# Weight pieces fetched three ahead of a conversion with two VectorE passes, in an attention and two-layer feed-forward kernel

## The chip, the cores and the metric

The kernel runs on one core of a Trainium2 chip. The metric is the device time of one execution in microseconds; lower is better. Three executions of the kernel before took 1069.86 to 1070.5 us, median 1070.43.

## The reference

The inputs are float32 for attention and float64 for the weights, as `_moe_setup` draws them (a float32 array divided by a numpy float64 scalar).

```python
scores = np.where(causal, -1e9, scale * q @ k.T)
a = np.exp(scores - scores.max(-1)); a /= a.sum(-1) + 1e-9
local = a @ v
q_p = phi(q)                                  # relu-like, elu(x) + 1
mem_out = (q_p @ M_prev) / (q_p @ z_prev + 1e-6)
x = g * mem_out + (1 - g) * local             # B=4, H=8, S=576, D=64
h = x @ w_in;  y = (h * cos(h)) @ w_out       # 2304 x 512, d_ff = 2048
h = y @ w_in2; out = (h * tanh(softplus(h))) @ w_out2
```

## The kernel before, in words

Attention is done for 16 pairs of heads (batch b, pair p), each in five steps of 128 rows of queries. A step has three stages that run two steps apart: `stage_a` (scores `sp` on TensorE for each of the two heads, mask and row maximum on VectorE at L240, exponential on ACT at L243, scaling on GpSimd at L265), `stage_b` (transposes `tp` and their copies `aT`) and `stage_c` (the sum `o`, whose high and low part go to DRAM as xsH and xsL). Both heads of a pair use one half of TensorE's rows each for `sp` and one half of its columns each for `o`. `prep` loads q, k, v and the memory of the next pair; `memory` makes the products `mp` and `mo`.

The feed-forward layers use products with high and low parts, three matmuls for one. Each layer's hidden width is cut into two halves, each half's weights stay in SBUF as float32r pairs: w0 (first layer, first half), w1, then w2 and w3 for the second layer. `ffn` alternates `first` (products `h`, L420) and `second` (products `y`, L478, L487). For the first half of the first layer, 256 tokens at a time, this work is spread over attention from the second batch on (L573 to L577), and x is read back from DRAM by `load_block` in tiles xbH and xbL.

The weights come as raw 8-byte numbers, in pieces of 128 x 512 (512 KB), 16 pieces for a half. `to_f32` (L121) loads a piece into one of two buffers `wst` and makes float32 of its two words, `lo` and `hi`: GpSimd scales `hi` (L119), ACT makes the three bits of `lo` (L128), and three VectorE passes put them together (L129, L130, L133). Then `load_half` (L146) makes the high part (`wh`, ACT or GpSimd in turn) and the low part (L163, GpSimd or VectorE in turn). `converted` (L556) takes the 16 pieces of w0 one after the other from attention step CONV0 = 14 on, 0.9 a step; the other 48 go beside the feed-forward stages.

The order on each engine is not the program's order: the tile framework lists the instructions by its own timeline when the kernel is built, and `tc.issue_after` holds some of them behind a marked instruction. SP issues all transfers from one queue, and one that waits for a free buffer holds up all behind it.

## Time and profile before

| what | value |
|---|---|
| median of 3 runs | 1070.43 us (1069.86 to 1070.5) |
| profiled execution, first to last instruction | 1068.0 us |
| around the span, median less span | 2.4 us |
| TensorE busy | 1042.6 us, 98% |
| VectorE, ACT, GpSimd busy | 490.7, 485.8, 391.6 us |
| moved by DMA | 116.99 MB, 110 GB/s over the span |

The profiled execution's own time is its span and the 2.4 us around it, 1070.4 us. Idle time of an engine counts only where TensorE, which is busy nearly always, waits for it. A group of instructions is named by source line, engine, operation and tiles; a mean can mix shapes.

### The profile page before, as it was taken

The numbers are of one execution on the slowest core, as the hardware profiler recorded it, in microseconds if no ns is written. First come the engines' busy times: TensorE is split into PE (matmuls) and PEld (weight loads), VectorE is DVE, ScalarE is ACT, GpSimd is POOL, SyncE is SP. The second block draws the span as 40 slices with busy tenths as digits, with TensorE's granted clock in tenths as the row PEclk, the third lists the DMA queues.
The fourth block names the chain that finished last, engine by engine and source line by source line (L and its number), as shares of the span: only waits on it lengthen the run. The fifth ranks groups of instructions, "written<-read, shape, count | busy, mean of one in ns | idle before, by whom it ended". The sixth has DMA issues, their size and how long they took to land.

```text
span 1068.0 us, 17139 instructions
## 1 busy us (share of the span) xinstructions
PE 1042.6 (98%) x6512; PEld 873.7 (82%) x6512; DVE 490.7 (46%) x1136; ACT 485.8 (45%) x1023; POOL 391.6 (37%) x425
## 2 busy tenths in 40 slices
PE   6997999999999999999999999999999999999998
PEld 4666688787878899998888889888888888888897
DVE  4588885445554558776766655665000000000000
ACT  6797875556564534344535454543322321222131
POOL 3377853323232334555555555654101010110100
PEclk8999999999999999999999999999999999999999
DMA  6366642323121275425345355630300300110010
GB/s 235 119 196 224 205 135 82 119 83 122 59 87 46 73 266 190 139 90 198 110 166 177 111 176 185 228 119 22 116 1 1 118 1 0 60 40 1 21 41 20
DMA packets 66369, 116.99 MB, mean 110 GB/s; under 512 B 5616, under 2 KB 25072, under 8 KB 66288
## 3 DMA queue, kind: packets, MB, share of 16 engines
q1 hardware_dynamic: 66288, 115.91, 32.2%
q8 instruction: 51, 0.84, 0.3%
q14 instruction: 30, 0.25, 0.1%
HBM read 87.58 MB, written 28.31 MB: 109 GB/s over the span
## 4 chain that ended last, share of the span: by engine, by line
PE 92%; ACT 2%; DVE 2%; DMA 2%; issue 1%; POOL 1%; SPq 0%; DVEq 0%; POOLq 0%; ACTq 0%
PE h L420 37%; PE y L478 20%; PE y L487 18%; PE o L324 5%; PE sp L238 4%; PE tp L297 4%; PE o L313 2%; PE mp L277 1%; PE sp L251 1%; DMA qt<-in_qp_dram 1%; DMA wst<-in_w1i_dram 1%; DVE at L240 1%; ACT at L243 1%; DMA vt<-in_vn_dram 1%; POOL at L265 0%
## 5 line engine op out<-in xcount | busy, mean ns | idle before, releaser
L420 PE MATMUL h<-xbH,w 128*128 128x256 f32 (+1 forms) x1536 | 393.0, 338 | 0.1
L420 PEld LDWEIGHTS h<-xbH,w 128*128 128x128 f32 x1536 | 266.9, 190 | 33.7 <-issue 1.0
L420 PE MATMUL h<-xbL,w 128*128 128x256 f32 (+1 forms) x768 | 258.0, 336 | 1.5 <-DMA xbL<-xsL 1.5
L478 PE MATMUL y<-g,w 128*128 128x256 f32 (+1 forms) x1344 | 221.5, 319 | 4.4 <-ACT aT L115 4.2
L478 PEld LDWEIGHTS y<-g,w 128*128 128x128 f32 x1344 | 193.1, 192 | 30.8 <-issue 9.4
L487 PE MATMUL y<-w,g 128*128 128x512 f32 x864 | 201.8, 389 | 0.0
L487 PEld LDWEIGHTS y<-w,g 128*128 128x128 f32 x864 | 161.9, 188 | 33.5
L392 DVE TENSOR_TENSOR g<-e,g 128x512 fp32r<-128x512 f32 x36 | 24.9, 691 | 297.1 <-ACT g L115 297.1
L420 PEld LDWEIGHTS h<-xbL,w 128*128 128x128 f32 x768 | 145.6, 190 | 16.9 <-DMA xbL<-xsL 1.7
L392 POOL TENSOR_TENSOR g<-e,g 128x512 fp32r<-128x512 f32 x36 | 47.8, 1328 | 286.5 <-ACT g L115 286.5
L265 POOL TENSOR_SCALAR at<-at,sm,omg 128x128 f32<-128x128 f32 (+2 forms) x144 | 102.7, 723 | 134.4 <-DVE sm L263 119.2
L384 ACT ACTIVATE e<-h 128x512 f32<-128x512 f32 x72 | 43.0, 597 | 232.5 <-PE h L420 231.0
L392 POOL TENSOR_TENSOR g<-u,g 128x512 fp32r<-128x512 f32 x72 | 102.0, 1436 | 121.5 <-ACT g L115 45.6
L367 ACT ACTIVATE u<-h 128x512 int32<-128x512 f32 x72 | 42.9, 595 | 111.9 <-PE h L420 104.2
L243 ACT ACTIVATE at<-at,mn 128x128 f32<-128x128 f32 (+3 forms) x128 | 70.9, 555 | 28.2 <-DVE mn L240 26.8
L129 DVE SCALAR_TENSOR_TENSOR wst<-wst 128x512 int32<-128x512 int32 x64 | 53.9, 843 | 37.7 <-POOL wst L119 31.3
L119 POOL TENSOR_SCALAR wst<-wst 128x512 f32<-128x512 f32 x64 | 46.4, 731 | 63.2 <-DMA wst<-in_w1i_dram 25.1
L297 PE MATMUL tp<-ident,at 128*128 128x128 f32 x384 | 63.9, 285 | 5.6 <-DVE den L281 2.2
L368 DVE SCALAR_TENSOR_TENSOR u<-u,h 128x512 f32<-128x512 int32 x72 | 49.0, 682 | 40.8 <-ACT u L367 40.5
L240 DVE CUSTOM_DVE_ANT_0 at<-sp,mask 128x128 f32<-128x128 f32 (+3 forms) x128 | 59.3, 482 | 17.6 <-PE sp L238 16.0
L133 DVE TENSOR_TENSOR wst<-wst 128x512 int32<-128x512 int32 x64 | 66.1, 1035 | 1.2
L324 PE MATMUL o<-aT,vt 128*64 128x128 f32 (+1 forms) x896 | 64.5, 272 | 1.7 <-ACT aT L115 1.5
(76 smaller groups left out, 1084.1 us busy)
## 6 DMA issues: line engine op xcount, KB each, us to landing
wst<-in_w1i_dram SPq DMA_DIRECT2D x16, 512.0 KB, 5.4
wst<-in_w1o_dram SPq DMA_DIRECT2D x16, 512.0 KB, 4.6
wst<-in_w2i_dram SPq DMA_DIRECT2D x16, 512.0 KB, 4.0
wst<-in_w2o_dram SPq DMA_DIRECT2D x16, 512.0 KB, 4.7
qd<-in_qT_dram SPq DMA_DIRECT2D x16, 320.0 KB, 3.4
vt<-in_vn_dram SPq DMA_DIRECT2D x16, 320.0 KB, 3.2
xbH<-xsH SPq DMA_DIRECT2D x20, 256.0 KB, 4.9
xbL<-xsL SPq DMA_DIRECT2D x20, 256.0 KB, 4.6
```

The costliest lines, as they stand in the source:

```text
L129: nc.vector.scalar_tensor_tensor(lo, hi, 3, lo, ALU.logical_shift_left, ALU.bitwise_or)
L133: nc.vector.tensor_tensor(dst, lo, hi, ALU.bitwise_xor)
L240: nc.vector.tensor_tensor_reduce(at[:, :N], sp[:, :N], mask[:, SM - q0:SM - q0 + N], SSC, 3.0e38, ALU.add, ALU.min, mn[:, j:j + 1])
L243: marks["act"] = nc.scalar.activation(at[:, :N], at[:, :N], AF.Exp, bias=mn[:, j:j + 1], scale=-1.0, accum_out=sm[:, j:j + 1]).ins
L265: turn_of("sc", b == 0).tensor_scalar(at[:, :N], at[:, :N], sm[:, j:j + 1], gates[j], ALU.mult, ALU.mult)
L297: nc.tensor.transpose(tp[:, c:c + P], at[:, c:c + P], ident)
L324: marks["pe"] = nc.tensor.matmul(o[j * D:(j + 1) * D, :n], st["vt"][:kk, c, j * D:(j + 1) * D], a, start=False, stop=c == i, skip_group_ch ...
L368: nc.vector.scalar_tensor_tensor(u, u.bitcast(I32), -TWO_PI, h, ALU.mult, ALU.add)
L392: turn_of(kind).tensor_tensor(gL, g, gH.bitcast(F32), ALU.subtract)
L420: nc.tensor.matmul(h[:, a * T:(a + 1) * T], w_[:, c, f0:f0 + P], x_[c], start=m == 0, stop=m == 3 * NC - 1)
L478: nc.tensor.matmul(y[e // per][:, cols], w_[:, f, es], g_, start=fst and m == 0 and e % per == 0, stop=lst and m == 2, skip_group_check=True)
L487: nc.tensor.matmul(y[t], g_[:, tsl], w_[:, f, :], start=fst and m == 0, stop=lst and m == 2, skip_group_check=True)
```

## The change

A piece is now fetched by `fetch` and converted by `to_f32`, and the generator of `load_half` runs three pieces ahead with its fetches; `wst` has four buffers. Fetches of w0 may start from attention step LOAD0 = 9. ACT's pass becomes a scaled copy that leaves the rounding in range without a clamp, and VectorE needs two passes: one takes the sign bit of `hi` into `lo`, one shifts `hi` by three and joins it. For w1 nothing is fetched ahead; for w2 three fetches stand at the start of the second half. The tiles xbH and xbL of the 256-token blocks become one ring of four places each (before, three buffers each), and 16 one-element memsets of the weight tiles go, with the constant 7.

```diff
@@ -19,11 +19,12 @@
 TWO_PI = 2.0 * math.pi
 BIG = 8.0e9
 BUFS = dict(
-    mb=2, kd=4, qd=4, aD=4, vt=2, qt=1, ph=2, den=2, mo=4, xH=1, xL=3, sm=7, mn=2, at=8, aT=7, u=2, e=3, g=4, h=4, y=4, xb=3, yp=3, yh=2, yl=2, wst=2, S=6, T=8,
+    mb=2, kd=4, qd=4, aD=4, vt=2, qt=1, ph=2, den=2, mo=4, xH=1, xL=3, sm=7, mn=2, at=8, aT=7, u=2, e=3, g=4, h=4, y=4, xb=3, xbH=4, xbL=4, yp=3, yh=2, yl=2, wst=4, S=6, T=8,
 )
 RES = 2
-TOUCH = 1
 CONV0 = 14
+LOAD0 = 9
+AHEAD = 3
 CONVR = 0.9
 PACE1 = 1.5
 PREP = 3
@@ -38,6 +39,7 @@
 
 
 REBIAS = 2.0 ** -112
+LOW = 29.0 / 32.0
 
 
 @with_exitstack
@@ -98,10 +100,16 @@
     nc.vector.reciprocal(gate, igate)
     nc.vector.tensor_scalar(omg, gate, -1.0, 1.0, ALU.mult, ALU.add)
 
-    c_seven = const.tile([P, 1], F32, name="c_seven")
-    nc.gpsimd.memset(c_seven, 7.0)
-
     counts = {}
+    rings = {}
+
+    def ring(pool, tag, shape, dtype=F32):
+
+        if tag not in rings:
+            rings[tag] = [pool.tile([shape[0], BUFS[tag], *shape[1:]], dtype, name=tag), 0]
+        r = rings[tag]
+        r[1] += 1
+        return r[0][:, (r[1] - 1) % BUFS[tag]]
 
     def turn_of(kind, first=False):
         kind += "0" if first else ""
@@ -118,20 +126,19 @@
         else:
             eng.tensor_scalar(dst, src, scale, 1.0, ALU.mult, ALU.mult)
 
-    def to_f32(src, dst=None):
-
-
+    def fetch(src):
         st = wk.tile([P, SM, 2], I32, tag="wst", name="wst", bufs=BUFS["wst"])
         nc.sync.dma_start(st, src)
+        return st
+
+    def to_f32(st):
+
         lo, hi = st[:, :, 0], st[:, :, 1]
         scaled("ws", hi.bitcast(F32), hi.bitcast(F32), REBIAS)
-        nc.scalar.activation(lo, lo.bitcast(U32), AF.Relu, scale=-(2.0 ** -29), bias=c_seven)
+        nc.scalar.activation(lo, lo.bitcast(U32), AF.Copy, scale=LOW * 2.0 ** -29, bias=0.2495)
+        nc.vector.scalar_tensor_tensor(lo, hi, -(1 << 31), lo, ALU.bitwise_and, ALU.bitwise_or)
         nc.vector.scalar_tensor_tensor(lo, hi, 3, lo, ALU.logical_shift_left, ALU.bitwise_or)
-        nc.vector.tensor_scalar(hi, hi, -(1 << 31), 7, ALU.bitwise_and, ALU.bitwise_or)
-        if dst is None:
-            dst = lo
-        nc.vector.tensor_tensor(dst, lo, hi, ALU.bitwise_xor)
-        return dst.bitcast(F32)
+        return lo.bitcast(F32)
 
     def weight_pieces(win, wout, half, tl):
 
@@ -143,15 +150,20 @@
         for f in range(f0 // P, f0 // P + 2):
             yield wo[:, f]
 
-    def load_half(pool, tagp, source, kind):
+    def load_half(pool, tagp, win, wout, half, kind, ahead=AHEAD):
         tiles = []
         for tl in range(NTL):
             tiles.append([pool.tile([P, NC, SM // 2] if k < 2 else [P, 2, DM], F32R, tag=f"{tagp}{k}{tl}", bufs=1,
                                     name=f"{tagp}{k}{tl}") for k in range(4)])
+        todo = [(tl, n, src) for tl in range(NTL) for n, src in enumerate(weight_pieces(win, wout, half, tl))]
 
         def gen():
-            for tl in range(NTL):
-                for n, t in enumerate(source(tl)):
+            raw = {}
+            for i in range(-ahead, len(todo)):
+                if i + ahead < len(todo):
+                    raw[i + ahead] = fetch(todo[i + ahead][2])
+                if i >= 0:
+                    tl, n, _ = todo[i]
                     k = n // 2 * 2
                     dH, dL = tiles[tl][k], tiles[tl][k + 1]
                     if k == 0:
@@ -159,16 +171,11 @@
                         dH, dL = (x[:, c:c + 2, :].rearrange("p c f -> p (c f)") for x in (dH, dL))
                     else:
                         dH, dL = (x[:, n - 2, :] for x in (dH, dL))
+                    t = to_f32(raw.pop(i))
                     scaled("wh", dH, t)
                     turn_of(kind).tensor_tensor(dL, t, dH.bitcast(F32), ALU.subtract)
-                    yield 0
+                yield i
         return tiles, gen()
-
-    def from_double(win, wout, half):
-        def f(tl):
-            for src in weight_pieces(win, wout, half, tl):
-                yield to_f32(src)
-        return f
 
     def drain(g):
         for _ in g:
@@ -460,7 +467,8 @@
             xs = ([], [])
             for c in range(0, NC, 2):
                 for n, l, d in (("xbH", xs[0], dH), ("xbL", xs[1], dL)):
-                    x = wk.tile([P, 2, size], F32R, tag=f"{n}{size}", name=n, bufs=BUFS["xb"])[:, :, :T]
+                    x = (ring(wk, n, [P, 2, size], F32R) if size < SM else
+                         wk.tile([P, 2, size], F32R, tag=n + "l", name=n, bufs=BUFS["xb"]))[:, :, :T]
                     src = d[c:c + 2, :, t0:t0 + T].rearrange("g p t -> p g t") if rearr else d[:, c:c + 2, t0:t0 + T]
                     nc.sync.dma_start(x.bitcast(F32), src)
                     l += [x[:, 0], x[:, 1]]
@@ -523,11 +531,7 @@
             nc.sync.dma_start(out[r:r + P, :], t)
 
 
-    w_a, ga = load_half(w0p, "w0", from_double(w1i, w1o, 0), "w0l")
-    if TOUCH:
-        for t in w_a:
-            for x in t:
-                nc.gpsimd.memset(x[:1, 0, :1].bitcast(F32), 0.0)
+    w_a, ga = load_half(w0p, "w0", w1i, w1o, 0, "w0l")
 
     def ends(us):
         return [(*u, i == 0, i == len(us) - 1) for i, u in enumerate(us)]
@@ -551,7 +555,7 @@
     m1 = ffn(m_pools, seq1, {0: w_a}, elem_cos("gh"), load_block(xsH, xsL, True, TB), mm2_t, fin_partial,
              lambda blk: sum(blk) <= stored[0] * S)
     k_done = 0
-    pieces = [0]
+    pieces = [-AHEAD]
 
     def converted(n):
         while pieces[0] < min(n, 4 * NTL):
@@ -559,6 +563,8 @@
             pieces[0] += 1
 
     for kind, s in at:
+        if kind == "a" and s >= LOAD0:
+            converted(min(s - LOAD0 + 1 - AHEAD, 0))
         if kind == "a" and s >= CONV0:
             with tc.issue_after(marks["act"]):
                 converted(int((s - CONV0 + 1) * CONVR))
@@ -576,21 +582,23 @@
             _, kk = next(m1)
             k_done = max(k_done, kk + 1)
     m_pools.append(psum("psX"))
-    w_b, gb = load_half(w1p, "w1", from_double(w1i, w1o, 1), "w1l")
+    w_b, gb = load_half(w1p, "w1", w1i, w1o, 1, "w1l", 0)
     with tc.issue_after(marks["pe"]), tc.issue_after(marks["sp"]):
         for _ in m1:
             next(gb, None)
         drain(gb)
     b_pools = [psum("psB")]
-    w_c, gc = load_half(w0p, "w2", from_double(w2i, w2o, 0), "w2l")
+    w_c, gc = load_half(w0p, "w2", w2i, w2o, 0, "w2l")
     m2 = ffn(b_pools, seq2, {1: w_b}, elem_cos("bh"), load_block(xsH, xsL, True), mm2_t, fin_full)
     with tc.issue_after(marks["sp"]):
         for i, _ in enumerate(m2):
+            if i < 2 * AHEAD and i % 2 == 0:
+                next(gc)
             if i % 4 == 1:
                 with tc.issue_after(marks["cos"]), tc.issue_after(last_sin[0]):
                     next(gc, None)
     drain(gc)
-    w_d, gd = load_half(w1p, "w3", from_double(w2i, w2o, 1), "w3l")
+    w_d, gd = load_half(w1p, "w3", w2i, w2o, 1, "w3l")
     with tc.issue_after(last_sin[0]):
         table = nc.scalar.preload_act_table_set("mish").ins
     m3 = ffn(b_pools, seq3, {0: w_c, 1: w_d}, elem_mish(), load_block(ysH, ysL, False), mm2_n, fin_out)
```

The change moves instructions on every engine. On SP, whose queue issues the loads, at the start of the program, before (q, k and v of a pair are qd, kd and vt, its memory mz, the second copy of q for the memory qt; wst is a weight piece):

```order
L206 DMA qd<-in_qT_dram 128x640
L204 DMA kd<-in_kT_dram 128x576
L95 DMA gate<-in_beta_dram 128x8
L215 DMA qt<-in_qp_dram 128x576
L209 DMA mz<-in_mbd_dram 128x130
L125 DMA wst<-in_w1i_dram 128x2x512
L212 DMA vt<-in_vn_dram 128x640
L209 DMA mz<-in_mbd_dram 128x130
L206 DMA qd<-in_qT_dram 128x640
L204 DMA kd<-in_kT_dram 128x576
L125 DMA wst<-in_w1i_dram 128x2x512
L212 DMA vt<-in_vn_dram 128x640
```

and with the change:

```order
L213 DMA qd<-in_qT_dram 128x640
L211 DMA kd<-in_kT_dram 128x576
L97 DMA gate<-in_beta_dram 128x8
L222 DMA qt<-in_qp_dram 128x576
L131 DMA wst<-in_w1i_dram 128x2x512
L216 DMA mz<-in_mbd_dram 128x130
L131 DMA wst<-in_w1i_dram 128x2x512
L131 DMA wst<-in_w1o_dram 128x1024
L219 DMA vt<-in_vn_dram 128x640
L213 DMA qd<-in_qT_dram 128x640
L211 DMA kd<-in_kT_dram 128x576
L131 DMA wst<-in_w1o_dram 128x1024
```

Four weight pieces stand among the first twelve loads in place of two, three of them ahead of the first vt. Behind these rows the load of qt for the second pair stands at the 16th place in both orders.

On ACT, where the conversion of w0 ends, before (at is an exponential of attention, L243; wst the bits of a piece, L128; w02 the high part of the last tile):

```order
L128 ACTIVATE wst_1566<-wst_1566,c_seven_88 128x512
L243 ACTIVATE at_1940,sm_1937<-at_1940,mn_1938 128x384
L262 ACTIVATE sm_1937<-sm_1937,c_eps_76 128x2
L217 ACTIVATE ph_2391<-qt_2389 128x576
L218 ACTIVATE ph_2391<-ph_2391 128x576
L328 ACTIVATE xH_1445<-o_1844 128x128
L115 ACTIVATE aT_1891<-tp_1890 128x512
L328 ACTIVATE xH_1445<-o_1917 128x128
L367 ACTIVATE u_1994<-h_1969 128x512
L115 ACTIVATE aT_1934<-tp_1933 128x128
L128 ACTIVATE wst_1612<-wst_1612,c_seven_88 128x512
L115 ACTIVATE w023_104<-wst_1566 128x512
```

and with the change:

```order
L250 ACTIVATE at_1567,sm_1565<-at_1567,mn_1566 128x256
L250 ACTIVATE at_1568,sm_1565<-at_1568,mn_1566 128x256
L138 ACTIVATE wst_1439<-wst_1439 128x512
L123 ACTIVATE aT_1500<-tp_1499 128x512
L269 ACTIVATE sm_1522<-sm_1522,c_eps_76 128x2
L224 ACTIVATE ph_1977<-qt_1975 128x576
L269 ACTIVATE sm_1565<-sm_1565,c_eps_76 128x2
L250 ACTIVATE at_1609,sm_1607<-at_1609,mn_1608 128x384
L335 ACTIVATE xH_1173<-o_1544 128x128
L225 ACTIVATE ph_1977<-ph_1977 128x576
L123 ACTIVATE w023_102<-wst_1373 128x512
```

The last high part stands behind 69 passes of attention's exponential before, and behind 59 with the change; the first conversion stands behind 29 in both. A pair of heads has nine such passes, so the 16 pieces lie in 4.4 pairs before and in 3.3 with the change.

On TensorE in the second pair of heads, before (sp are scores, one head each; x2 in a row are both heads):

```order
L313 MATMUL o<-ident,mo 128x128
L324 MATMUL o<-aT,vt 64x128 x8
L238 MATMUL sp<-kd,qd 128x512
L297 MATMUL tp<-ident,at 128x128 x2
L313 MATMUL o<-ident,mo 128x64
L238 MATMUL sp<-kd,qd 128x512
L251 MATMUL sp<-kd,qd 128x512
L324 MATMUL o<-aT,vt 64x64 x8
L324 MATMUL o<-aD,vt 64x64 x2
L297 MATMUL tp<-ident,at 128x128 x4
```

and with the change, at the same pair:

```order
L245 MATMUL sp<-kd,qd 128x128 x2
L245 MATMUL sp<-kd,qd 128x256 x2
L245 MATMUL sp<-kd,qd 128x384 x2
L245 MATMUL sp<-kd,qd 128x512 x2
L284 MATMUL mp<-mz,ph 128x130 x5
L320 MATMUL o<-ident,mo 128x128
L331 MATMUL o<-aT,vt 64x128 x6
L304 MATMUL tp<-ident,at 128x128 x4
L310 MATMUL td<-ident,at 64x128
```

The two heads' scores of 512 columns stand apart before and together with the change (the x1 row of L251 is the fifth step's, which has all rows). The first product h stands behind 58 products sp and sd before and behind 68 with the change. From the product h that stands behind the last 16 of the first y products on, the two orders on TensorE are the same up to the last pairs of attention.

## Rows read from the trace of the kernel before

**Rows 1.** The page: busy time of each engine.
```profile
PE 1042.6 (98%) x6512; PEld 873.7 (82%) x6512; DVE 490.7 (46%) x1136; ACT 485.8 (45%) x1023; POOL 391.6 (37%) x425
```

**Rows 2.** Busy time by stage: stretch, length, busy and (instructions) of each engine, clock, DMA.
```profile
core 0: us, PE busy (x) PEld busy (x) DVE busy (x) ACT busy (x) POOL busy (x), PEclk, DMA share, GB/s
16.00:23.60 7.60, 6.40 (x32) 4.56 (x33) 2.39 (x9) 4.92 (x13) 0.55 (x1) 0.55 0.54 181
23.60:58.00 34.40, 34.40 (x267) 22.41 (x266) 20.79 (x91) 27.68 (x91) 11.50 (x19) 1.00 0.39 126
58.00:140.00 82.00, 73.73 (x618) 55.36 (x617) 72.32 (x231) 65.70 (x183) 64.55 (x72) 0.98 0.60 197
140.00:162.70 22.70, 22.70 (x195) 18.61 (x194) 17.20 (x54) 15.25 (x37) 10.64 (x12) 1.00 0.44 136
162.70:372.00 209.30, 205.12 (x1729) 171.02 (x1729) 107.38 (x369) 118.99 (x302) 63.36 (x84) 0.99 0.27 85
480.00:700.00 220.00, 220.00 (x1062) 186.02 (x1062) 142.57 (x171) 104.04 (x154) 123.48 (x102) 1.00 0.48 167
```

**Rows 3.** Waits of TensorE, 162.7 to 372 us: total, times, longest.
```profile
PE y L478 <- ACT aT L115: 4.2, 3, 1.4
```

**Rows 4.** Waits of TensorE, 58 to 140 us.
```profile
PE tp L297 <- DVE den L281: 2.2, 1, 2.2
PE h L420 <- DMA xbL<-xsL: 1.5, 1, 1.5
...
```

**Rows 5.** Chain of waits, 86 to 108 us: start, length, what.
```profile
91.73 6.65 DMA wst<-in_w1i_dram
...
98.47 0.78 ACT wst L128
...
104.83 0.80 PE o L313 x2
```

**Rows 6.** Busy time by stage, two more stretches.
```profile
58.00:98.00 40.00, 37.30 (x309) 27.78 (x308) 33.51 (x109) 31.73 (x95) 32.40 (x38) 1.00 0.69 230
104.00:107.00 3.00, 2.17 (x16) 1.95 (x18) 3.00 (x8) 1.99 (x4) 2.12 (x2) 0.64 0.33 98
```

**Rows 7.** Groups of VectorE, 58 to 140 us: count, busy, mean ns, idle before.
```profile
L240 DVE CUSTOM_DVE_ANT_0 at<-sp,mask 128x384 f32<-128x384 f32 (+3 forms) x33 | 15.4, 480 | 1.2 <-PE sp L238 1.2
L133 DVE TENSOR_TENSOR wst<-wst 128x512 int32<-128x512 int32 x14 | 11.1, 794 | 0.1
L129 DVE SCALAR_TENSOR_TENSOR wst<-wst 128x512 int32<-128x512 int32 x14 | 10.2, 728 | 2.8 <-POOL wst L119 2.3 <-ACT wst L128 0.6
L130 DVE TENSOR_SCALAR wst<-wst 128x512 int32<-128x512 int32 x14 | 8.7, 620 | 0.0
...
L163 DVE TENSOR_TENSOR w<-wst,w 128x512 fp32r<-128x512 f32 x7 | 4.9, 700 | 1.2 <-POOL w L119 1.2
```

**Rows 8.** Tile wst: shortest, median and longest ns of L129, whole trace.
```profile
L129 DVE SCALAR_TENSOR_TENSOR wst<-wst x64: 674/686/1795, 56.6 to 734.4; 128x512 int32<-128x512 int32 x64
```

**Rows 9.** Chain of waits: memory products of two pairs that follow each other.
```profile
23.61 1.12 PE mp L277 x10
...
40.97 1.12 PE mp L277 x10
```

**Rows 10.** Chain of waits: scores (512 columns) and o products, alone or both heads.
```profile
46.85 1.05 PE sp L238 x2
...
50.62 0.37 PE o L324 x4
...
138.01 0.36 PE o L324 x2
...
140.31 1.12 PE sp L238 x4
```

**Rows 11.** Transfers, 0 to 40 us: GB/s in 40 slices of 1 us.
```profile
GB/s 0 36 273 328 98 257 362 352 386 404 403 414 403 394 386 396 391 379 300 113 194 0 0 0 16 0 0 23 248 345 24 0 0 0 0 203 343 231 369 83
```

**Rows 12.** Timeline of the start: start, length, what [idle before].
```profile
16.18 0.68 ACT L217 ACTIVATE ph<-qt 128x576 f32<-128x576 f32 x1 [1.45 <-DMA qt<-in_qp_dram]
...
17.80 0.69 PE L324 MATMUL o<-aT,vt 128*64 128x128 f32 x2 [1.20 <-ACT aT L115]
```

## Prediction

> **What bounds the kernel now.** I began with the busy times of the page: TensorE is busy for 1042.6 of 1068.0 us [rows 1], so the change can only win back what TensorE loses, 25 us, and what it does at half clock. Second, the table by stage [rows 2] shows where that is. From 480 to 700 us TensorE has no idle time at all, although weight pieces are converted there too; what becomes cheaper or earlier there is worth nothing. From 162.7 to 372 us it idles for 4.2 us, all in three waits of the y products for an ACT copy [rows 3]. The rest lies ahead of 162.7 us: the first 16 us, in which the first tiles arrive, then 1.2 us and a clock of 0.55 up to 23.6, nothing up to 58, and 82.00 - 73.73 = 8.3 us from 58 to 140. In that last stretch, where the first 16 weight pieces are converted beside attention, VectorE is busy 72.3 of 82 us, ACT 65.7 and GpSimd 64.6.
>
> Third, the longest waits of TensorE in this stretch [rows 4] name DVE den (2.2) and a DMA of xbL (1.5). Fourth, the chain of waits [rows 5] shows what lies behind the first: a weight transfer issued at 91.73 lands at 98.38, ACT's conversion pass stands in its queue ahead of attention's exponentials, and TensorE is whole again only at 104.83. The clock then is 0.64 for 3 us [rows 6], between the levels of 1.2 and 2.4 GHz.
>
> The baseline of the sum is the span of 1068.0 us plus the 2.4 us that the runs show around it, 1070.4; the median of the runs is 1070.43.
>
> **Passes and transfers.** A piece costs VectorE three passes now: L129, L130 and L133, at 728, 620 and 794 ns in this stretch [rows 7], plus L163 at 700 ns for every second piece. The change drops L130 and makes L133 a pass like L129. I price both new passes at 728 ns, the row of the same operation on the same operands; the bounds are its 674 and 1795 ns [rows 8]. So a piece goes from 0.73 + 0.62 + 0.79 + 0.35 = 2.49 us to 0.73 + 0.73 + 0.35 = 1.81 us of VectorE. ACT's Relu becomes a Copy over the same elements, taken at the same price; GpSimd keeps its passes and loses 16 memsets that nobody waits for. All of that is worth nothing by itself, since the 48 later pieces are hidden [rows 2].
>
> The row of L129 reaches 1795 ns where 674 ns is possible [rows 8], and GpSimd is busy most of that time. The Trainium skill ("SBUF — State Buffer", section "Who interferes with whom" and the summary around it) says that a VectorE instruction with two SBUF inputs and a GpSimd one that reads SBUF block each other for the whole instruction. By that rule the change drops a pass with one input and keeps two exposed ones: at the maximum of the row they would cost 2 x 1.8 us, and the burst of the next paragraph would be VectorE's alone. The row agrees that it happens, and its mean of 728 ns says that here it is rare.
>
> **The hole and the burst.** With four buffers and fetches three pieces ahead, the wait of 6.65 us is gone, and so is that for xbL, whose four loads now stand together ahead of the next weights. But the order shows that the scheduler spends the cheaper passes on pace: 16 pieces over 3.3 pairs of heads instead of 4.4, 4.8 a pair instead of 3.6, and no h product among them. What VectorE has to do for a pair does not fall. From 58 to 140 us it runs 33 of the L240 passes [rows 7], of which a pair has 8: 4.1 pairs, and 72.3/4.1 = 17.6 us a pair. Of these 14/4.1 x 2.49 = 8.5 are conversion; with 4.8 x 1.81 = 8.7 in their place it has 17.8. TensorE's attention takes 17.4 us a pair where nothing stops it, from one memory product to the next [rows 9], and about 16.3 with one more score product of 512 columns beside its other head. If VectorE runs at 100%, TensorE loses (17.8 - 16.3) x 3.3 = 5 us in the burst; at the 88% of now, (20.2 - 16.3) x 3.3 = 13 us; if the passes fall into gaps, as from 140 to 162.7 us, where TensorE loses nothing beside a VectorE at 76% [rows 2], about 1 us. I take 5.5, the share of time lost now (8.3 of 82, 10%) on a burst of 3.3 x 17 = 56 us, and keep 1 and 13. What goes is the 8.3 us and the half clock of rows 2 (2% of 82, 1.6 us): 9.9. Net: **5.5 - 9.9 = -4.4**, from -8.9 to +3.1. Behind the burst all h products stand close together, as from 140 to 162.7 us, where TensorE has no idle time [rows 2].
>
> **Heads together.** A score product of one head alone holds TensorE as long as both heads side by side: 1.05 us alone, 1.12 for two, at 512 columns [rows 10]; likewise 0.36 alone and 0.37 for two of the o products. Up to the point from which the two orders agree (162.7 us now), I counted separated pairs of heads: at 512, 384, 256 and 128 columns 3, 2, 3 and 3 before, and 1, 2, 1 and 4 after. With 1.05 us in proportion to the columns that is 7.1 against 4.2 us. Of the o products 6 pairs are separated before and 9 after, +1.1 us. Net: **-1.8**, between -2.9 and 0 (0 where ACT, at 27.7 of 34.4 us, takes over).
>
> **The start.** Four pieces of 512 KB now stand among the first twelve transfers, where there were two. The transfers are what TensorE waits for there: 380 to 410 GB/s from 8 to 17 us [rows 11]. The load of q for the second pair, which ACT waits for until 16.18 [rows 12], has two weight pieces more ahead of it and one q and one k load less, 416 KB or 1.1 us at 390 GB/s. It held all four aT copies, and TensorE until 17.80; in the new order the first copy stands ahead of it, and three transposes move into the wait (0.9 us). Bounds: -0.9, and +2.7 for both pieces in full. I take **+0.5**, between the two orders' effects.
>
> That the transfers share one rate is in the row: 1 MB more is 2.7 us at 390 GB/s. The Trainium skill ("DMA: Bandwidth & Descriptors", section "Issuing engines are not separate DMA queues") says why no reordering gets around it: all queues run on the same 16 engines. By it alone the start would cost the full +2.7, and the sum would be 1066.9; the row of the wait at 16.18 says that only what stands ahead of that one load counts.
>
> Later stages: from 162.7 us on the two orders agree on TensorE up to the end of attention, so the three waits [rows 3] stay, 0. The conversions from 372 us stay under TensorE's own work; if that cover went, they would be late by single passes of 0.7 us.
>
> **Sum:** 1070.4 - 4.4 - 1.8 + 0.5 = 1064.7 us.
>
> **Rivals.**
> *The passes no longer bind.* If the burst costs 1 us rather than 5.5, the time is 1060.2. For it: nothing in VectorE's queue is long and the transfers are in place. Against it: ACT and GpSimd are at 80% too.
> *No gain: the burst takes all back.* The burst at 88% (13 us) and heads together half in vain where ACT binds: 1070.4 + 3.1 + 0.5 - 0.9 = 1073.1 at worst; with 9 us for the burst 1070.4 - 0.9 - 0.9 + 0.5 = 1069.1, the value I give it. Here also belongs that the change doesn't do what it says: the fifth fetch still waits for the first buffer, which is released by the same conversion as before, and stands in SP's queue behind other loads. The hole then stays in part.
> *Slower: half clock in the burst.* Gaps of 2 us took the clock down at 104 [rows 6] and at the start, where 7.6 us ran at 0.55 [rows 2], a loss of 3.4 us. In the burst there are no h products to fill TensorE's queue. If VectorE holds it off for 9 us in gaps like these and the clock falls twice, the time is 1070.4 - 9.9 + 9 + 2 x 3.4 - 1.8 + 0.5 = 1075.0. [...]
>
> **How the numbers follow.** The forecast has 0.52, passes that no longer bind 0.14, no gain 0.22, half clock 0.12. A measurement can tell about 0.2%, 2.1 us. The first two are faster: 0.66; no gain lies within: 0.22; half clock is slower: 0.12. The forecast's own range, with bounds of its terms not all at one end, is 1061 to 1068. The range that should hold 8 in 10 is 1059.5 to 1071.5: it takes in the deep gain at 1060.2 and most of no gain, and leaves out half clock and a few per cent at each end. The predicted time is 1064.7.
>
> **What would show it.** In the profile after: no wait of ACT or GpSimd for a wst transfer from 50 to 140 us; two passes a piece of about 0.7 us; all 16 pieces done by about 120 us, where now 14 spread over 58 to 140; TensorE's idle time from 58 us to the point where the orders agree 4 to 7 us, now 8.3; that point reached near 157 us instead of 162.7; the three waits of 1.4 us unchanged; the clock near 1.00 from 58 to 140. TensorE's first o product later than 18.5 us would show the start as mis-sized. It is wrong if TensorE idles for 9 us or more in the burst, or if the clock falls there.

## The result, and the profile after

The kernel with the change takes 1078.2 us (median of 6 runs, 1075.8 to 1081.39) against 1071.26 us (6 runs) of the kernel before on the same chips: 1.0065 of it, interval 1.0047 to 1.0084. Faster was forecast, 1064.7 us; it is 7 us slower, and outside the range.

Busy time by engine, on the page of the kernel after:

```profile
PE 1044.8 (97%) x6512; PEld 878.1 (82%) x6512; DVE 466.8 (43%) x1072; ACT 478.9 (44%) x1023; POOL 405.3 (38%) x408
```

Against [rows 1] VectorE has 24 us less to do, and GpSimd 14 us more, although all that changed in its instructions is that 17 memsets are gone: its conversion passes became longer. TensorE has the same 6512 products and is out of work for 32 us instead of 25. Two of the stretches of [rows 2], and two later ones, of the kernel after (columns as there):

```profile
58.00:140.00 82.00, 72.11 (x570) 53.74 (x568) 70.11 (x206) 58.60 (x167) 62.31 (x66) 0.92 0.56 184
...
162.70:372.00 209.30, 205.13 (x1742) 171.02 (x1742) 107.39 (x369) 118.94 (x302) 64.41 (x87) 1.00 0.27 86
372.00:480.00 108.00, 104.70 (x853) 102.68 (x850) 76.79 (x101) 39.69 (x60) 60.35 (x53) 0.97 0.54 184
...
700.00:900.00 200.00, 198.89 (x875) 163.60 (x874) 31.93 (x37) 56.68 (x94) 41.18 (x34) 1.00 0.13 43
```

From 58 to 140 us TensorE idles 9.9 us where it idled 8.3, at a clock of 0.92 where it had 0.98 (means over parts at full and at half clock). From 372 to 480 us, where it idled 0.25 us at full clock (below), it idles 3.3 us at 0.97; from 700 to 900 us 1.1 us, before nothing. The kernel before, from 372 to 480 us:

```profile
372.00:480.00 108.00, 107.75 (x892) 105.56 (x889) 75.11 (x118) 42.07 (x63) 49.99 (x50) 1.00 0.50 169
```

GpSimd is busy 10 us longer there now. To lay the two traces over each other I number TensorE's 6512 products by their start. From the point where the two orders on TensorE come together (162.7 us before; below, the merge point) the n-th is the same product or a close neighbour; ahead of it, it only says how much work is done. Product 1200 stands for the merge point. How much later it starts than in the kernel before, in us (the column heads give its start in that kernel; this table goes on through the experiments):

| kernel | product 400 (65.2) | 1200 (169.0) | 3300 (421.8) | 3900 (512.9) | 5100 (764.5) | median of the runs |
|---|---|---|---|---|---|---|
| after | -3.2 | +1.6 | +0.1 | +5.8 | +7.9 | 1078.2 |
| two passes alone | +0.5 | +5.7 | +4.2 | +9.8 | +12.4 | 1082.1 |
| fetch ahead, three passes | -2.9 | +3.3 | +1.8 | +9.9 | +17.7 | 1088.1 |
| two passes and an idle one | +1.9 | +4.4 | +2.9 | +10.9 | +12.6 | 1079.8 |
| pace 0.6 | -2.5 | -4.3 | -4.3 | +2.1 | +6.0 | 1073.5 |
| GpSimd relieved in the burst | -2.6 | -4.7 | -6.2 | +0.9 | +5.0 | 1075.3 |
| w1 thin | -1.7 | +1.7 | +0.2 | -0.6 | +6.5 | 1074.4 |
| no GpSimd for w1 to w3 | -2.1 | +3.5 | +3.5 | +2.7 | +2.7 | 1069.2 |
| two buffers for w1 to w3 | -2.8 | -0.8 | -2.3 | -3.0 | -3.0 | 1067.8 |
| even in all places | -3.7 | -6.8 | -6.8 | -5.6 | -5.6 | 1064.7 |
| relieved and even | -3.1 | -1.8 | -1.8 | -1.4 | -1.4 | 1067.2 |
| relieved, two buffers later | -3.7 | -3.1 | -3.2 | -3.9 | -3.9 | 1065.3 |
| pace 0.6, two buffers later | -3.0 | -5.4 | -6.9 | -7.6 | -7.6 | 1063.0 |

So the first 65 us lost nothing (3.2 us ahead), and the loss lies in three places: **the burst** up to the merge point (4.8 us between products 400 and 1200), **w1's conversion** near 440 us (5.7 us) and **w3's** near 700 us (2.1 us, of which 1.1 are idle time). The merge point itself, in the timeline of TensorE of the kernel after; before it was at 162.68:

```profile
164.27 0.28 PE L427 MATMUL h<-xbH,w 128*128 128x256 f32 x1
```

**The burst.** Four shorter stretches of the kernel after:

```profile
58.00:70.00 12.00, 11.80 (x78) 7.21 (x77) 11.77 (x34) 10.81 (x37) 12.00 (x12) 1.00 0.68 237
70.00:81.00 11.00, 7.36 (x44) 6.13 (x43) 8.18 (x24) 7.61 (x22) 10.28 (x13) 0.69 0.66 215
96.00:104.00 8.00, 4.00 (x28) 3.18 (x26) 6.42 (x14) 4.63 (x11) 7.16 (x8) 0.79 0.87 322
113.00:121.00 8.00, 6.39 (x38) 4.59 (x39) 8.00 (x20) 5.30 (x15) 7.08 (x8) 0.79 0.03 7
```

Three gaps, each with a lower clock at or behind it: (1 - 0.69) x 11 + 2 x (1 - 0.79) x 8 = up to 6.8 us on top of the idle time. Counted up to product 1200, TensorE idles 18.9 us (before 17.3) and is busy at half clock for 17.3 us (before 9.0). If half of that busy time is lost, the clock costs 8.7 us (before 4.5), and what is left of TensorE's own work is 143.1 us (before 147.2). By this estimate the +1.6 us at the merge point are 1.6 more of idle time and 4.1 more by the clock, less 4.1 that the new order saves TensorE.

GpSimd is busy without a break ahead of the first. The chain of waits there (start, length, what):

```profile
65.83 1.07 POOL wst L127
66.90 1.70 POOL w L176
68.60 0.68 POOL at L272
...
70.97 0.64 POOL w L127
71.61 0.86 POOL at L272
...
72.92 0.64 POOL wst L127
73.55 1.29 POOL at L272 x2
...
74.86 1.09 PE tp L304 x4
```

Conversion passes (wst, w) stand between attention's scalings (at) in GpSimd's queue, and TensorE's transposes wait for the scalings. GpSimd's groups in the kernel after from 58 to 121 us (count, busy, mean ns, idle before):

```profile
L272 POOL TENSOR_SCALAR at<-at,sm,omg 128x128 f32<-128x128 f32 (+4 forms) x30 | 29.2, 981 | 6.6 <-DVE sm L270 6.6
L176 POOL TENSOR_TENSOR w<-wst,w 128x512 fp32r<-128x512 f32 x8 | 11.3, 1410 | 0.5 <-ACT w L123 0.5
L127 POOL TENSOR_SCALAR wst<-wst 128x512 f32<-128x512 f32 x12 | 10.4, 876 | 3.8 <-DMA wst<-in_w1o_dram 3.8
L127 POOL TENSOR_SCALAR w<-wst 128x512 fp32r<-128x512 f32 x8 | 7.0, 879 | 0.6 <-DVE wst L140 0.6
```

The conversion is as much work for GpSimd as attention is. VectorE is busy for 58.1 of these 63 us and GpSimd for 56.4, so busy time alone does not say which of them binds. The second gap is the old hole of [rows 5], nearly as long:

```profile
90.73 6.02 DMA wst<-in_w1o_dram
...
97.58 1.13 DVE wst L139
...
99.23 0.68 DVE w L176
...
100.00 0.46 DVE mo L289
...
100.59 0.72 PE o L320 x2
```

In the same chain the fetch follows two issues of x loads (L473) on SP, which had waited for a store of x. The deeper ring doesn't help a fetch that stands behind something else. What TensorE waited for from 50 to 170 us, largest first:

```profile
PE o L320 <- DVE mo L289: 4.0, 1, 4.0
PE tp L304 <- POOL at L272: 3.3, 1, 3.3
PE o L320 <- DVE mn L247: 1.5, 1, 1.5
```

**w1, near 440 us.** The waits of TensorE in the kernel after from 372 to 480 us:

```profile
PE y L486 <- POOL g L399: 2.2, 1, 2.2
PE y L486 <- DVE yp L125: 1.1, 1, 1.1
```

and GpSimd's timeline, where the layer's own products g stand with a conversion pass ahead of each:

```profile
438.67 0.77 POOL L127 TENSOR_SCALAR wst<-wst 128x512 f32<-128x512 f32 x1 [1.35 <-DMA wst<-in_w1o_dram]
439.40 1.69 POOL L399 TENSOR_TENSOR g<-u,g 128x512 fp32r<-128x512 f32 x1
441.06 0.83 POOL L127 TENSOR_SCALAR wst<-wst 128x512 f32<-128x512 f32 x1
441.86 1.69 POOL L399 TENSOR_TENSOR g<-u,g 128x512 fp32r<-128x512 f32 x1
```

The pass ahead of the first g had itself waited 1.35 us for its transfer, and g stands behind it in the queue. In the kernel before the two g of a step stood together, 2.57 us for both:

```profile
438.00 2.57 POOL L392 TENSOR_TENSOR g<-u,g 128x512 fp32r<-128x512 f32 x2 [2.85 <-DVE g L117]
```

From the start of the first g to the end of the second it is 4.15 us now; of the 1.6 us more about half is the pass between them, and half that each g takes longer. The waits of 3.3 us stand in a stretch of 14 us at a clock of 0.76, which is up to 0.24 x 14 = 3.4 us more:

```profile
436.00:450.00 14.00, 10.70 (x66) 10.30 (x65) 14.00 (x17) 5.56 (x9) 11.11 (x11) 0.76 0.50 154
```

VectorE is busy without a break there, GpSimd 11.1 of 14 us. And the conversion that was to be cheaper hardly was. Tile wst on VectorE from 372 to 480 us (shortest, median, longest ns), kernel after:

```profile
L139 DVE SCALAR_TENSOR_TENSOR wst<-wst x17: 678/771/1841, 385.9 to 448.0; 128x512 int32<-128x512 int32 x17
L140 DVE SCALAR_TENSOR_TENSOR wst<-wst x17: 678/1034/1823, 388.5 to 449.7; 128x512 int32<-128x512 int32 x17
```

and before:

```profile
L129 DVE SCALAR_TENSOR_TENSOR wst<-wst x17: 674/695/1795, 385.9 to 479.7; 128x512 int32<-128x512 int32 x17
L130 DVE TENSOR_SCALAR wst<-wst x16: 415/424/769, 388.5 to 475.5; 128x512 int32<-128x512 int32 x16
L133 DVE TENSOR_TENSOR wst<-wst x16: 678/689/1690, 389.3 to 476.0; 128x512 int32<-128x512 int32 x16
```

Many passes take about 0.68 us and many well over 1 us, so a median can jump from one group to the other. By the means of the same passes a piece takes 0.99 + 1.15 = 2.1 us in two passes and took 1.01 + 0.47 + 0.83 = 2.3 us in three: 0.2 us less, where the prediction had 0.7 less. The 16 pieces of w1 are put together by 448 us instead of 477.

### The profile page after: what moved, and what is told of

It reads as the page before. It is cut to its first block, busy times and chain, and to the rows that moved or that the text cites. A ratio compares the mean times of both kernels' runs of the same rounds, so it can differ in the third digit from the quotient of the medians.

```text
span 1076.7 us, 17062 instructions
## 1 busy us (share of the span) xinstructions
PE 1044.8 (97%) x6512; PEld 878.1 (82%) x6512; DVE 466.8 (43%) x1072; ACT 478.9 (44%) x1023; POOL 405.3 (38%) x408
## 4 chain that ended last, share of the span: by engine, by line
PE 83%; DVE 5%; POOL 4%; ACT 4%; DMA 2%; issue 2%; SPq 0%; DVEq 0%; POOLq 0%; ACTq 0%
PE h L427 33%; PE y L486 17%; PE y L495 16%; PE o L331 5%; PE tp L304 3%; PE sp L245 3%; DVE wst L139 2%; PE o L320 2%; DVE wst L140 1%; PE mp L284 1%; DMA wst<-in_w1o_dram 1%; ACT at L250 1%; POOL at L272 1%; POOL w L176 1%; PE sp L258 1%
## 5 line engine op out<-in xcount | busy, mean ns | idle before, releaser
L127 POOL TENSOR_SCALAR wst<-wst 128x512 f32<-128x512 f32 x64 | 54.8, 861 | 74.1 <-DMA wst<-in_w1i_dram 24.0
L140 DVE SCALAR_TENSOR_TENSOR wst<-wst 128x512 int32<-128x512 int32 x64 | 71.9, 1128 | 0.7
L331 PE MATMUL o<-aT,vt 128*64 128x128 f32 (+1 forms) x896 | 66.8, 275 | 0.2 <-ACT aT L123 0.2
L139 DVE SCALAR_TENSOR_TENSOR wst<-wst 128x512 int32<-128x512 int32 x64 | 61.1, 956 | 8.0 <-POOL wst L127 7.3
```

What stands on the lines that cost most here:

```text
L127: eng.tensor_scalar(dst, src, scale, 1.0, ALU.mult, ALU.mult)
L139: nc.vector.scalar_tensor_tensor(lo, hi, -(1 << 31), lo, ALU.bitwise_and, ALU.bitwise_or)
L140: nc.vector.scalar_tensor_tensor(lo, hi, 3, lo, ALU.logical_shift_left, ALU.bitwise_or)
L331: marks["pe"] = nc.tensor.matmul(o[j * D:(j + 1) * D, :n], st["vt"][:kk, c, j * D:(j + 1) * D], a, start=False, stop=c == i, skip_group_ch ...
```

## The experiments

All are timed beside the kernel before on one chip; the ratio is to it. Two theories ran through them: that the pieces stand **denser in the in-order queues**, ahead of passes that TensorE needs, because four buffers let them; and that the **two passes are slow in themselves**, each with two operands in SBUF, beside GpSimd.

**The halves of the change alone.** The kernel before with the new conversion:

```diff
-        nc.scalar.activation(lo, lo.bitcast(U32), AF.Relu, scale=-(2.0 ** -29), bias=c_seven)
-        nc.vector.scalar_tensor_tensor(lo, hi, 3, lo, ALU.logical_shift_left, ALU.bitwise_or)
-        nc.vector.tensor_scalar(hi, hi, -(1 << 31), 7, ALU.bitwise_and, ALU.bitwise_or)
-        nc.vector.tensor_tensor(dst, lo, hi, ALU.bitwise_xor)
+        nc.scalar.activation(lo, lo.bitcast(U32), AF.Copy, scale=LOW * 2.0 ** -29, bias=0.2495)
+        nc.vector.scalar_tensor_tensor(lo, hi, -(1 << 31), lo, ALU.bitwise_and, ALU.bitwise_or)
+        nc.vector.scalar_tensor_tensor(lo, hi, 3, lo, ALU.logical_shift_left, ALU.bitwise_or)
...
```

> The kernel before with the two-pass conversion alone; two raw buffers, no fetch ahead. Theory (four buffers let the conversion stand denser in the queues of GpSimd and VectorE, ahead of the passes that TensorE waits for): no such gap here, time as before within 2 us, no half clock at 73, 100, 117 or 442 us. Rival (the two passes with two operands each are slow beside GpSimd and hold both engines): slower than before by 3 us or more, although nothing stands denser.

1082.08 us, ratio 1.0086 (1.0058 to 1.0114). A miss for the theory, and by its time the rival's case: about as slow as the whole change (the intervals overlap), with two buffers and the old pace. The chain of waits before its gap near 468 us:

```profile
466.32 0.60 DVE wst L130
466.92 1.44 DVE g L118
...
469.82 6.19 PE y L476 x30
```

A conversion pass stands ahead of the layer's cast g, and the cast takes 1.44 us, beside GpSimd's pass on a piece. It is the same kind of place as in the kernel after, reached without the four buffers.

The change with the old conversion, the reverse of that edit on the other kernel:

```diff
-        nc.scalar.activation(lo, lo.bitcast(U32), AF.Copy, scale=LOW * 2.0 ** -29, bias=0.2495)
-        nc.vector.scalar_tensor_tensor(lo, hi, -(1 << 31), lo, ALU.bitwise_and, ALU.bitwise_or)
+        nc.scalar.activation(lo, lo.bitcast(U32), AF.Relu, scale=-(2.0 ** -29), bias=c_seven)
         nc.vector.scalar_tensor_tensor(lo, hi, 3, lo, ALU.logical_shift_left, ALU.bitwise_or)
+        nc.vector.tensor_scalar(hi, hi, -(1 << 31), 7, ALU.bitwise_and, ALU.bitwise_or)
+        nc.vector.tensor_tensor(lo, lo, hi, ALU.bitwise_xor)
```

> The changed kernel with the old conversion of three VectorE passes; four buffers, fetches three ahead. Theory (density of the queues): as slow as the changed kernel or slower, 1077 to 1083 us, with the wait for GpSimd's product near 442 us. Rival (the slow two passes): back to the time of before or better, under 1072 us.

1088.09 us, ratio 1.0147 (1.0112 to 1.0183): the worst of all, as the theory had it, though by more: both later places lose (8.1 and 7.8 us in the table). With four buffers a third pass makes the later places worse; the cheaper conversion is worth 9 us there by the two ratios, and is not what slows the change.

The two passes and a third that nothing needs:

```diff
+        nc.vector.tensor_scalar(hi, hi, -(1 << 31), 7, ALU.bitwise_and, ALU.bitwise_or)
         return lo.bitcast(F32)
```

> The kernel before with the two-pass conversion and a third VectorE pass that nothing needs, so that the build counts as much VectorE work a piece as before. Theory (it is the order, built from cheaper passes, that made the two passes alone 10 us slower): most of it comes back, 1070 to 1075 us. Rival (the two passes with two operands are slow in themselves beside GpSimd): still 1080 us or more, since they are all there and one pass is added.

1079.75 us, ratio 1.0084 (1.0062 to 1.0106), between the bounds of the two. Meant to bring the old order back, it did not: TensorE waits 5.1 us for the cast g at the same place near 468 us. So it tells the theories apart less than it should; what in the built order of these two kernels differs enough from the kernel before stays open.

**The burst.** Pace:

```diff
-CONVR = 0.9
+CONVR = 0.6
```

> The changed kernel with 0.6 weight pieces a step of attention instead of 0.9; the 16 pieces of w0 lie over 40 passes of the exponential instead of 29. Theory: GpSimd is no longer busy without a break, the waits of 3.3 to 4.0 us from 69 to 117 us shrink under 2 us, at most one stretch of half clock is left between 58 and 140 us, and the merge point comes 3 to 5 us earlier: 1073 to 1075 us. Rival (start and transfers cost it): unchanged at 1078 us.

1073.52 us, ratio 1.0011 (0.9997 to 1.0026). The merge point lies 4.3 us ahead of the kernel before, 5.9 us ahead of the change; TensorE's longest wait from 50 to 170 us is 1.3 us. The later places lose more than with the change (6.4 and 3.9 us for 5.7 and 2.1). The stretch from 58 to 140 us:

```profile
58.00:140.00 82.00, 77.24 (x624) 54.96 (x621) 74.80 (x227) 64.08 (x187) 64.31 (x72) 0.96 0.60 196
```

TensorE idles 4.8 us in place of 9.9. So the pace makes the burst dear.

GpSimd relieved:

```diff
-    w0l="pv", ..., wh="ap"
+    w0l="v", wh0="a", ..., wh="ap"
-                    scaled("wh", dH, t)
+                    scaled("wh", dH, t, first=kind == "w0l")
```

> The changed kernel, w0's low parts all on VectorE and its high parts all on ACT: GpSimd keeps one pass a piece, and loses 8 of 1.3 to 1.7 us and 8 of 0.65 us. Theory (in the burst it is GpSimd that TensorE waits for): the wait of 3.3 us for the scaled probabilities at 71 us goes, the merge point comes 2 us or more earlier, 1074 to 1076 us. Rival (VectorE is what binds, as the prediction priced it): VectorE has 8 passes more, the merge point 2 to 4 us later, 1080 to 1082 us.

1075.3 us, ratio 1.0046 (1.0028 to 1.0063). The merge point comes 6.3 us earlier than with the change, at the full pace of 0.9, and with 8 passes more on VectorE; the wait of 3.3 us is gone, and the longest one left is 1.3 us. The later places lose 7.0 and 4.2 us, so that the interval of the whole time still overlaps with the change's. The stretch from 58 to 140 us:

```profile
58.00:140.00 82.00, 74.61 (x619) 53.81 (x616) 74.15 (x235) 67.75 (x193) 51.79 (x56) 1.00 0.58 193
```

VectorE has 4 us more, GpSimd 10.5 less, and the clock stays at 1.00. VectorE, with more to do, wasn't what bound the burst; what GpSimd had to do was.

**The later places.** w1 as thin as before:

```diff
-        for _ in m1:
-            next(gb, None)
+        for kind, _ in m1:
+            if kind == "m1":
+                with tc.issue_after(marks["cos"]), tc.issue_after(last_sin[0]):
+                    next(gb, None)
```

> The changed kernel, where the pieces of w1 are spread as thinly as before, over 15 products instead of 9, each behind the cosine passes. Theory: the waits of the y products for GpSimd (2.2 us) and VectorE (1.1 us) near 440 us go, with the half clock that stands behind them (6.8 us at half, 3.4 us lost): 1078.2 - 5.6 = 1072.6 us. Rival (slow passes): still there somewhere, 1077 us or more.

1074.38 us, ratio 1.0029 (1.0013 to 1.0045). Near 440 us nothing is lost any more: it gains 0.8 us from product 3300 to 3900, where the change lost 5.7. But near 700 us it loses 7.0 us, where the change lost 2.1 with the same order on every engine there:

```profile
PE h L427 <- ACT e L391: 4.5, 2, 2.5
```

The Mish e stands on ACT behind a high part w that waits for VectorE's passes. That part of the total was missed.

Two raw buffers for all but w0:

```diff
+    ..., wst=4, wsu=2, ...
...
-        st = wk.tile([P, SM, 2], I32, tag="wst", name="wst", bufs=BUFS["wst"])
+        st = wk.tile([P, SM, 2], I32, tag=tag, name="wst", bufs=BUFS[tag])
...
-                    raw[i + ahead] = fetch(todo[i + ahead][2])
+                    raw[i + ahead] = fetch(todo[i + ahead][2], "wst" if kind == "w0l" else "wsu")
```

> The changed kernel with four raw buffers for w0 alone, and two of their own for w1, w2 and w3. Theory (four buffers let the later pieces stand denser): what is lost near 440 and 700 us goes: 1078.2 - 5.6 - 2.1 = 1070.5 us. Rival (the cheaper passes alone rearrange the queues so that something is late, as in the run with the two passes alone, 5.6 us near 468 us and 2.6 us near 740 us): 1077 to 1080 us.

1067.78 us, ratio 0.9975 (0.9963 to 0.9987): faster than before, with the order of the change in the burst. Nothing is lost later: no wait of TensorE shows from 372 to 800 us. VectorE's passes from 372 to 480 us:

```profile
L139 DVE SCALAR_TENSOR_TENSOR wst<-wst x17: 675/693/1781, 383.7 to 460.4; 128x512 int32<-128x512 int32 x17
L140 DVE SCALAR_TENSOR_TENSOR wst<-wst x17: 678/694/1804, 386.3 to 462.1; 128x512 int32<-128x512 int32 x17
```

The medians are short again, but by the means a piece still takes 0.91 + 1.05 = 2.0 us, against 2.1 with the change. The two passes alone, which lost 5.6 and 2.6 us with the same number of buffers, take 1.02 + 0.95 = 2.0 us there as well. So neither the length of the passes nor the number of buffers decides by itself what is lost. What is left is where the passes stand in the queues. The built orders of these two runs do differ there on VectorE, ACT and GpSimd; which of the differences decides isn't shown.

No GpSimd in the conversions of w1 to w3:

```diff
-    sc="p", ws="p", w0l="pv", w1l="vp", w2l="vp", w3l="vp", ...
-    wh="ap", ...
+    sc="p", ws0="p", wh0="ap", ws="a", w0l="pv", w1l="v", w2l="v", w3l="v", ...
+    wh="a", ...
...
```

> The changed kernel, where the conversions of w1, w2 and w3 leave GpSimd: its scaling and high parts go to ACT, its low parts to VectorE. Theory one (passes of GpSimd and VectorE hold each other up): VectorE's passes fall from 1.0 to 1.8 us to 0.7 us there, and what was lost near 440 and 700 us comes back: 1078.2 - 5.6 - 2.1 = 1070.5 us. Theory two (what stands deep in an in-order queue ahead of the layer's own passes): ACT's queue now holds three passes a piece ahead of the layer's own, waits stay or grow, 1077 to 1085 us.

1069.16 us, ratio 0.9984 (0.9971 to 0.9996), as theory one had it. The pieces are as dense as in the change (the last of w1 ends at 446 us), ACT has all the more ahead of its own passes, and yet nothing is lost behind product 3300:

```profile
372.00:480.00 108.00, 108.00 (x908) 106.36 (x907) 69.31 (x110) 54.12 (x85) 24.07 (x19) 1.00 0.54 184
...
L139 DVE SCALAR_TENSOR_TENSOR wst<-wst x17: 677/683/1790, 389.6 to 447.3; 128x512 int32<-128x512 int32 x17
L140 DVE SCALAR_TENSOR_TENSOR wst<-wst x17: 675/684/1783, 391.9 to 449.1; 128x512 int32<-128x512 int32 x17
```

By the means a piece takes 0.83 + 0.78 = 1.6 us. So density costs by way of GpSimd. By which of two ways, this run can't tell: it shortens VectorE's passes, and it also takes the pieces out of GpSimd's queue, where one of them stood ahead of each product g near 440 us. The two passes alone, with passes no longer than those of the run with two later buffers, speak against length as the only cause.

That passes of the two engines fall on each other is plain all the same. The Trainium skill ("SBUF — State Buffer", section "Who interferes with whom") states that a VectorE instruction with two SBUF inputs and a GpSimd one that reads SBUF exclude each other for a whole instruction. The trace agrees: in the kernel after, 16 of the 128 passes L139 and L140 have no GpSimd instruction beside them, and they take 0.68 to 0.69 us; 63 take over 1.0 us, up to 1.84, and each of these ends 0.53 to 0.56 us after a GpSimd instruction ends, as if its work began only then.

**Put together.** Pace 0.6, w1 thin, and w3 one piece for each product, behind its Mish:

```diff
...
+        for _ in range(AHEAD):
+            next(gd)
-        for i, _ in enumerate(m3):
-            next(gd, None)
-            next(gd, None)
+        for kind, _ in m3:
+            if kind == "m1":
+                with tc.issue_after(marks["e"]):
+                    next(gd, None)
```

> The changed kernel, spread evenly in all three places: 0.6 pieces a step in attention, w1 over 15 products as in the run with w1 slow, w3 one piece for each product of the second layer, behind its Mish. Theory (density): merge point 4.3 us ahead of the kernel before, nothing lost near 440 and 700 us: 1064 to 1067 us. Rival (the loss near 700 us has another cause than density): 1068 to 1073 us.

1064.7 us, ratio 0.9947 (0.993 to 0.9963): inside the theory's bounds, with the merge point 6.8 us ahead of the kernel before. Of that it loses 1.2 us later.

The same with GpSimd relieved in the burst and pace 0.7:

> The changed kernel with GpSimd relieved in the burst (w0's low parts on VectorE, its high parts on ACT), 0.7 pieces a step, and w1 and w3 spread evenly. Theory (GpSimd binds the burst, density the later places): 5 to 8 us ahead at the merge point, nothing lost later, 1061 to 1065 us. Rival (relief and slower pace take away the same gap, so that only one counts, and the even spread at 440 us depends on where the burst ends): 1065 to 1070 us.

1067.19 us, ratio 0.996 (0.9947 to 0.9974): the rival. Relief and slower pace take away the same gap, and do not add: the merge point is 1.8 us ahead, less than with either alone (4.7 and 4.3), since other gaps, of 2.5 and 2.0 us, came instead.

Relief at pace 0.9, with two later buffers:

> The changed kernel with GpSimd relieved in the burst, at 0.9 pieces a step, and two raw buffers of their own for the later pieces. Theory: 4.7 us ahead at the merge point as in the run with GpSimd relieved, and nothing lost later as in the run with two later buffers: 1070.4 - 4.7 - 2 = 1064 us, between 1062 and 1066. Rival (what happens later depends on when the burst ends, not on the buffers): 1068 to 1076 us.

1065.3 us, ratio 0.9943 (0.9926 to 0.9961), inside the theory's bounds, though the merge point is 3.1 us ahead and not 4.7.

Pace 0.6 with two later buffers:

> The changed kernel with 0.6 pieces a step in attention and two raw buffers of their own for w1, w2 and w3. Theory (pace binds the burst, the four buffers the later places, and the two add up): merge point 4 to 7 us ahead of the kernel before, and nothing lost near 440 and 700 us as in the run with two later buffers: 1063 to 1066 us. Rival (the later places depend on where the burst ends, as in the run at pace 0.6 with four buffers, where 1.5 and 1.0 us waits came near 650 to 740 us): 1068 to 1073 us.

1063.02 us, ratio 0.9922 (0.9908 to 0.9937): the fastest, 7.7 us under the kernel before. It is the change with two edits: `CONVR = 0.6`, and two buffers for w1 to w3. Beside the run with two later buffers alone, where nothing is lost later either, the last two runs give what the burst costs in whole times: the ratio falls from 0.9975 to 0.9943 with GpSimd relieved and to 0.9922 with the slower pace, both outside its interval. The stretches of the run at pace 0.6:

```profile
58.00:140.00 82.00, 77.04 (x621) 54.87 (x622) 74.54 (x224) 63.78 (x185) 63.81 (x72) 0.98 0.60 194
...
372.00:480.00 108.00, 108.00 (x856) 105.37 (x851) 74.11 (x103) 43.81 (x65) 57.77 (x53) 1.00 0.58 192
...
700.00:900.00 200.00, 200.00 (x884) 165.67 (x883) 26.77 (x32) 53.77 (x88) 37.49 (x32) 1.00 0.13 43
```

## Why the prediction was wrong

- **The start: no sign of a mis-sizing; heads together: at least as good as forecast.** Forecast +0.5 and -1.8. The o product that an ACT copy held until 17.80 us [rows 12] starts at 17.62 us; the first o product of all, L320, comes at 16.93 us, 1.0 us later than before. By the estimate above TensorE's own work up to the merge point became 4.1 us shorter; no run separates the two terms.
- **"5.5 us" for the burst: wrong, the step that failed first.** 5.5 - 9.9 = -4.4 us was forecast; from product 400 to 1200 the change lost 4.8. The step reckoned VectorE's work for a pair, at 728 ns a pass, and took the share of time that TensorE lost before. From 58 to 121 us the two passes have means of 942 and 874 ns, and GpSimd, whose work for a pair the step left out, is busy without a break ahead of the first gap. With GpSimd relieved and 8 passes more on VectorE the merge point came 6.3 us earlier, so the bound that the step had named is not the one that held. The term for the clock, 1.6 us to be won back, had the wrong sign: up to the merge point the clock costs 4.1 us more, by the estimate above. The rival "half clock in the burst" (chance 0.12) described that, though for gaps that VectorE makes.
- **"The wait of 6.65 us is gone": wrong.** A wait of 6.02 us is there, since the fetch stands in SP's queue behind loads of x. This was named among the ways to no gain, and not priced.
- **"The scheduler spends the cheaper passes on pace": wrong cause.** Counted on ACT, the first passes of w0's 16 pieces lie over 41 exponentials with the two passes alone, 32 with the fetch ahead alone, 29 with both. Before it was 40. So it is mostly the fetch ahead that sets the pace.
- **"The conversions from 372 us stay under TensorE's own work", priced at 0: the second step that failed.** It overlooked that `wst` has four buffers there too, although w1 is not fetched ahead. The pieces of w1 stand over 9 products instead of 14, and the losses are 5.7 us near 440 and 2.1 near 700. No rival had them. The two buffers of their own take both away.
- **The rule on shared ports, weighed and called rare: misjudged.** A mean of 728 ns from the thin order of the kernel before says little of a dense one, and [rows 7] had a sign against "rare": L133 had a mean of 794 ns there, and the dropped L130, with one input, 620 ns, where its shortest passes near 440 us take 415. So the dropped pass was lengthened too. From 372 to 480 us the two passes took 2.1 us a piece, three had taken 2.3.
- **The three waits of the y products up to 372 us: as forecast**, 4.2 us both times; but the half clock behind one of them, near 204 us ([rows 2], 0.99), is not there now (1.00), which gives 1.5 us back between products 1200 and 3300.

The sum of what happened: +1.6 at the merge point, -1.5, +5.7, +2.1 = +7.9 at the last products, and 0.8 us more behind the last of them: 8.7 us between the two spans.

## What to carry to other kernels

Price a burst on every engine that takes part in it, with the longest queue as the bound; an engine that is busy 80% of a stretch on average can be the one that is busy without a break where it matters. A deeper ring acts wherever its tag is used: ask what else it lets move forward, and give a ring of its own to the stage that needs it. When passes of VectorE and GpSimd are packed closer, don't take their durations from the loose order.

## What the runs showed that I had not expected

- Short gaps of TensorE are dear here: at 440 us two waits of 3.3 us together became 5.7 us, since the clock was 0.76 over the 14 us around them. In the kernel before, the granted clock was 0.50 from 204 to 207 us, right behind a single wait of 1.4 us; in the kernel after, the same wait was followed by none of it.
- One built order is not one time: in the burst the kernel after and the runs with w1 thin, without GpSimd later and with two later buffers have the same order on TensorE and nearly so elsewhere, and their merge points lie 1.6, 1.7, 3.5 and -0.8 us from the kernel before. A gain of 2 us in one place of one profile is not yet a finding. The six runs with a slower pace or with GpSimd relieved lie 1.8 to 6.8 us ahead there, all of them ahead of these four.
- Neither half of the change alone is faster than the kernel before (1.0086 and 1.0147, both together 1.0065). Up to the merge point the two passes alone lose 5.7 us: by the count used above 0.6 of it is idle time, 2.7 the clock, and 2.4 TensorE's own work, which became longer in the order that was built for them. What in the passes led to that order was not settled.
